# The PSUM bank kept for transposed k becomes a fourth shared bank, and the order of all instructions is made anew

## The chip, the cores and the metric

The kernel runs on one core of a Trainium2 chip. A core has five engines, each with its own queue of instructions that it works off strictly in order: TensorE (PE in the profile, with its weight loads as PEld), VectorE (DVE), ScalarE (ACT), GpSimd (POOL) and SyncE (SP), which here only issues DMAs. Matrix products are written to PSUM, which has eight banks of 128 partitions by 512 floats; DVE and ACT read them there. The metric is the time of one execution on the device in microseconds (us).

## The reference

Two stages follow each other for 4 sequences (B) of 768 tokens (S). The first is a recurrence over tokens with 8 heads of 48 elements, the second a gated feed-forward layer with a product over the sequence. Cut to what matters:

```python
for t in range(S):                                    # first stage, per head
    cur = einsum('bhd,bhe->bhde', u[None] * kt, vt)
    y[:, :, t] = einsum('bhd,bhde->bhe', rt, state + cur)
    state = wt[:, :, :, None] * state + einsum('bhd,bhe->bhde', kt, vt)

h = gelu(x @ w_in)                                    # x is y, (B, 768, 384); w_in 384 x 1024
u, v = h[..., :512], h[..., 512:]
v_n = (v - mean(v)) / sqrt(var(v) + 1e-06) * g_ln
v_s = einsum('ts,bsd->btd', w_sg, v_n) + b_sg[None, :, None]
return x + (u * v_s) @ w_out                          # w_out 512 x 384
```

## The kernel before, in words

The recurrence is cut into chunks of 128 tokens (`C`), six per sequence, 24 in all, numbered 0 to 23 in this text. For each chunk DVE runs two scans over the decay factors (`decays`, lines 445 and 450), DVE or POOL multiplies them into r and k (lines 452 and 474), PE transposes k (`turned_k`, line 521) and multiplies (`products`, lines 535 and 538), DVE masks the result (`masked`, line 556) and adds up the state (`state`, lines 571 and 579), and PE makes the chunk's output from both (`outputs`, lines 618 and 642). Line 592 or, on ACT, line 590 decays the state between chunks. `own_weights` gives the weight of each token for itself: from products on PE for the first six chunks (line 488), from two multiplications and a sum (lines 496, 498, 501) for the others; line 510 or, on ACT, line 508 spreads it over a diagonal.

The feed-forward layer needs its left factors in two parts, high and low, so each product is three matmuls (lines 721, 722 and 723). It goes by half sequences of 384 tokens: `split_x` makes the two parts of x (on PE with lines 710 and 711 for the first chunks, else by a subtraction in line 716), `v_piece` one product per chunk of 128 tokens, then GELU and the normalisation (lines 744 to 763), `u_piece` four products per half, `gate_piece` four products per half over all six chunks of v (weights `wsgh`, `wsgl`), each followed by DVE, DVE, ACT, DVE (lines 797, 799, 801, 803), and `out_piece` three products per half from the four gates. Weights come as 64-bit words; `f64_weight` splits them on DVE, and for the first ones also on PE (lines 856 to 858).

Every product that fills a PSUM bank takes one from the pool `m_m` (tiles `m_ps`) and gives it back when its last reader is done: a `v` or `u` product after the GELU on ACT, a gate product after line 803, an out product after line 819. The pool holds three banks before. Two banks belong to `a_ps`, two to `y_ps`, and one, `k_ps`, to the transposed k alone:

```python
    m_a = slots("a_ps", 1, [2, FF], at=ps)
    m_s = slots("k_ps", 1, [NP, C], at=ps)
    m_y = slots("y_ps", 1, [2, 256], [2, 256], at=ps)
    m_m = slots("m_ps", 3, [FF], at=ps)
```

The order of instructions on each queue is not written out. Each step is a generator that yields `Op`s, and `Plan.run` places them one after the other on the engine where they would end first, by assumed costs (`Op({"DVE": 0.6, "POOL": 1.15}, ...)` lets the planner choose), by the ranks of the steps (`LEAD`, `FIRST`, `PIECE`, `WEIGHT`) and by which buffers are free by its clock. An `Op` with `two=True` on DVE excludes POOL in the plan, and the reverse. What comes out is a fixed order on each queue and a fixed choice of engine and bank; on the chip only semaphores between producers and consumers hold instructions back.

Of the kernel before, what the change touches and what calls it, by code (L numbers as in the profile page):

```python
# [36 lines left out]
LEAD = (2.27, 1.56, 2.02, 2.02)  # L37
FIRST = {"v": -0.61, "u": 5.2, "gate": 4.9, "out": 9.02}
PIECE = {"v": 1.09, "u": 7.07, "gate": 7.71, "out": 2.93}
WEIGHT = {"v": -4.46, "u": -19.4, "sg0": 2.89, "sg1": 2.21, "out": -10.09, "g": 17.79}  # L40

BIAS = {"DVE": -0.0, "POOL": -0.09}
JOINED = 6

ON_PE = {"own": 6, "x": 5, "w": 8}
# [49 lines left out]
class Event:  # L95
    t = None
# [194 lines left out]
def rwkv_gmlp(ctx: ExitStack, tc: tile.TileContext, wpad, kr, vtok, ktok, vt, u, ucol, w_in, g_ln, w_sgT, b_sg, w_out, out):  # L291
    nc = tc.nc
# [4 lines left out]
    def copy(e, o, i):  # L297
        nc.scalar.copy(o, i) if e == "ACT" else engine[e].tensor_copy(o, i)  # L298
# [141 lines left out]
    def decays(n):  # L440

        x = ch[n]
        yield Op({"DVE": 1.15}, after=[x.e_W], done=x.e_suf, two=True)
        W, Suf = x.W, x.Suf
        nc.vector.tensor_tensor_scan(Suf[:, WL - 1:0:-1], W[:, WL - 1:0:-1], D1[:, WL - 1:0:-1], 0.0,  # L445
                                     ALU.mult, ALU.add)
        yield Op({"DVE": 0.12}, after=[ch[n - 1].e_pre] if n else [])
        nc.vector.reciprocal(D2[:, 0:WL - 1:Q], Suf[:, 1:WL - 1:Q])
        yield Op({"DVE": 1.15}, done=x.e_pre, two=True)
        nc.vector.tensor_tensor_scan(W[:, 0:WL - 1], W[:, 0:WL - 1], D2[:, 0:WL - 1], 0.0, ALU.mult, ALU.add)  # L450
# [20 lines left out]
    def decayed_k(n):  # L471
        x = ch[n]
        op = yield Op({"DVE": 0.6, "POOL": 1.15}, after=[x.e_KR, x.e_suf, *x.own], done=x.e_k, two=True)
        engine[op.e].tensor_tensor(cols(x.KR[:, 0]), cols(x.KR[:, 0]), blocks(x.Suf, 2), ALU.mult)
        x.w.done(op.seen)

    def own_weights(n):
# [15 lines left out]
        else:  # L493
            op = yield Op({"POOL": 1.05, "DVE": 0.47}, after=[x.e_RK, e_u], two=True)
            t = x.rk.tile
            engine[op.e].tensor_tensor(t[:, 0], t[:, 0], u_bc, ALU.mult)
            op = yield Op({"POOL": 1.05, "DVE": 0.47}, two=True)
# [4 lines left out]
        op = yield Op({"POOL": 1.0, "ACT": 1.92, "DVE": 0.6}, take=[s_a], done=x.e_A, free=[own], two=True)  # L502
# [10 lines left out]
    def turned_k(n):  # L513

        x = ch[n]
        m = T if steps[n][1] == NC - 1 else C
        op = yield Op({"PE": 0.37}, after=[x.e_k, *([ch[n - 1].e_kt] if n else [])], take=[m_s])
        kt_ps, = op.got
        x.kr.done(op.seen)
        for p in range(NP):  # L520
            nc.tensor.transpose(kt_ps.tile[0:m, p], x.KR[:, 0, p * C:p * C + m], ident)
# [36 lines left out]
    def state(n):  # L558
# [5 lines left out]
        op = yield Op({"DVE": 0.27} if g else {"DVE": 0.27, "ACT": 0.3}, after=[x.e_sd, *([x.e_S2] if g else [])],  # L564
# [9 lines left out]
        if not last:  # L574
            op = yield Op({"DVE": 0.27}, take=[s_S1], done=x.e_S1)
            x.S1, = op.got
            x.ps.done(op.seen)
            x.T2.done(op.seen)
            nc.vector.tensor_tensor(x.S1.tile, ds_ps(1), x.T2.tile[:, :, 0:D], ALU.add)

    def decayed(n):

        x, before = ch[n], ch[n - 1]
        op = yield Op({"DVE": 0.27, "POOL": 0.6, "ACT": 0.92}, after=[before.e_S1, x.e_pc], take=[s_S2], done=x.e_S2,
# [21 lines left out]
    def outputs(n):  # L606
# [29 lines left out]
        op = yield Op({"PE": 0.79 if g else 0.55}, small=True, after=[e_look, *final], done=x.e_ym, next_to=joined)  # L636
# [58 lines left out]
    def split_x(h_, g):  # L695
# [19 lines left out]
        op = yield Op({"DVE": 0.46, "POOL": 1.05}, done=h_.e_x[g], free=[h_.x], two=True)  # L715
# [9 lines left out]
    def v_piece(b, g):  # L725
# [29 lines left out]
        op = yield Op({"ACT": 0.85, "DVE": 0.46, "POOL": 0.95}, free=[sb])  # L755
# [74 lines left out]
    def f64_weight(src, hi, lo, done, rank, at, after, on_pe):  # L830
# [9 lines left out]
        yield Op({"DVE": 0.38 if n == FF else 0.3}, two=True)  # L840
# [9 lines left out]
        yield Op({"DVE": 0.59 if n == FF else 0.48}, free=[b_raw], two=True)  # L850
        nc.vector.scalar_tensor_tensor(lo if on_pe else f, words(raw, U32, 0), 2.0 ** -52, f, ALU.mult, ALU.mult)
        if on_pe:
            op = yield Op({"PE": 1.4 if n == FF else 1.1}, take=[m_m], after=[e_hi], free=[b_t])
# [29 lines left out]
    def f32_weight(src, hi, lo, done, after):  # L883
# [5 lines left out]
        op = yield Op({"POOL": 1.05, "DVE": 0.47}, done=done, free=[raw], two=True)  # L889
# [89 lines left out]
    cnt_ps = m_s.take().tile[0:1, 0, 0:1]  # L979
# [175 lines left out]
```

## Time and profile before

| what | us |
|---|---|
| median of 3 runs (lowest, highest) | 376.29 (375.42, 378.51) |
| the profiled execution | 379.16 |
| its span, first to last instruction | 377.5 |
| PE busy in the span | 350.0 (93%) |
| DVE busy | 288.7 (76%) |
| ACT busy | 190.9 (51%) |
| POOL busy | 88.3 (23%) |

Times in all tables and rows below are those of the one profiled execution, which was slower than the median. A row of the groups of instructions reads: line, engine, operation, tile written <- tiles read, shapes, count, then busy us, mean ns of one, and the idle time of its engine just before them. A row of the waits reads: engine, line, the engine and line waited for, us in total, times, the longest. PE's count of fp32 matmuls is two for one instruction of lines 488, 535, 538, 618, 642, 710 and 856, because each runs in two passes.

### The profile page before, as it was taken

What the parts mean: (1) busy time and instruction counts of PE and PEld (TensorE: products, weight loads), DVE (VectorE), ACT (ScalarE), POOL (GpSimd) and SP (SyncE); (2) the same over time, 40 slices, a digit from 0 to 9 for tenths busy, and PEclk for the clock granted to TensorE, in tenths of its full rate; (3) what the DMA queues carried; (4) which work ended last, traced back from release to release, by engine and by line L of the source; (5) the groups of instructions that cost most, each with busy time, mean ns of one, the idle gap of its engine ahead of it and who ended that gap; (6) DMA issues with size and microseconds to landing.
All of it is one profiled execution on the core that took longest, in us unless ns stands there. A gap on an engine that the chain in (4) does not pass through costs nothing.

```text
span 377.5 us, 10936 instructions
## 1 busy us (share of the span) xinstructions
PE 350.0 (93%) x4505; PEld 317.8 (84%) x4505; DVE 288.7 (76%) x577; ACT 190.9 (51%) x508; POOL 88.3 (23%) x118
## 2 busy tenths in 40 slices
PE   1988899998999998999986999999999999999994
PEld 1665768797998888899986988899999889999993
DVE  7999999999999999999988797675531655353151
ACT  2566886882544575874353156663246764411210
POOL 7121331224252364143402314230000122100000
PEclk9999999999999999999999899999999999999999
DMA  8686754681165436753355412140145501001001
GB/s 257 256 268 185 226 176 143 202 303 62 47 234 159 156 129 198 259 178 103 120 155 181 123 51 84 65 158 15 57 175 180 173 3 63 3 0 63 2 0 70
DMA packets 23961, 49.82 MB, mean 132 GB/s; under 512 B 3808, under 2 KB 12768, under 8 KB 23904
## 3 DMA queue, kind: packets, MB, share of 16 engines
q1 hardware_dynamic: 23904, 49.05, 39.5%
q8 instruction: 37, 0.61, 0.6%
q14 instruction: 20, 0.16, 0.1%
HBM read 43.14 MB, written 4.72 MB: 127 GB/s over the span
## 4 chain that ended last, share of the span: by engine, by line
PE 43%; DVE 22%; DMA 3%; issue 2%; ACT 1%; DVEq 0%; ACTq 0%
PE m_ps L721 13%; PE m_ps L723 12%; PE m_ps L722 12%; DVE W L445 3%; DVE xT L716 2%; DVE m_ps L797 2%; DVE W L450 2%; DMA KR<-in_w_in 2%; DVE a L556 1%; PE y_ps L618 1%; DVE vn L763 1%; DMA out<-o 1%; DVE own L501 1%; PE y_ps L642 1%; DVE m_ps L799 1%
## 5 line engine op out<-in xcount | busy, mean ns | idle before, releaser
L721 PE MATMUL m_ps<-wsgh,vn 128*128 128x384 f32 x192 | 66.5, 347 | 1.9 <-DVE g L803 1.9
L723 PE MATMUL m_ps<-wsgh,vn 128*128 128x384 f32 x192 | 65.8, 343 | 0.4 <-DVE vn L763 0.4
L722 PE MATMUL m_ps<-wsgl,vn 128*128 128x384 f32 x192 | 65.5, 341 | 0.0
L801 ACT CAST g<-m_ps 128x384 fp32r<-128x384 f32 x32 | 15.3, 479 | 63.3 <-DVE m_ps L799 63.3
L721 PEld LDWEIGHTS m_ps<-wsgh,vn 128*128 128x128 f32 x192 | 36.6, 191 | 3.1 <-DVE g L803 2.5
L797 DVE SCALAR_TENSOR_TENSOR m_ps<-m_ps,g_ln,b_bc 128x384 f32<-128x384 f32 x32 | 19.7, 620 | 25.5 <-PE m_ps L723 25.3
L723 PEld LDWEIGHTS m_ps<-wsgh,vn 128*128 128x128 f32 x192 | 36.6, 190 | 1.1 <-DVE vn L763 1.1
L722 PEld LDWEIGHTS m_ps<-wsgl,vn 128*128 128x128 f32 x192 | 36.5, 190 | 0.2
L721 PE MATMUL m_ps<-xT,winh 128*128 128x384 f32 x96 | 34.3, 357 | 0.0
L721 PE MATMUL m_ps<-g,wouth 128*128 128x384 f32 x96 | 33.3, 347 | 0.4 <-ACT v L744 0.4
L722 PE MATMUL m_ps<-g,wouth 128*128 128x384 f32 x96 | 32.5, 339 | 0.8 <-DVE g L803 0.8
L722 PE MATMUL m_ps<-xT,winh 128*128 128x384 f32 x96 | 32.4, 338 | 0.0
L723 PE MATMUL m_ps<-xT,winl 128*128 128x384 f32 x96 | 32.4, 338 | 0.0
L723 PE MATMUL m_ps<-g,woutl 128*128 128x384 f32 x96 | 32.4, 338 | 0.0
L461 ACT ACTIVATE junk<-W 128x1032 f32<-128x1032 f32 x24 | 25.6, 1067 | 13.0 <-DVE W L450 8.0
L445 DVE TENSOR_TENSOR_SCAN W<-W,D 128x516 f32<-128x516 f32 x24 | 30.9, 1286 | 1.7 <-DMA W<-in_wpad 1.7
L450 DVE TENSOR_TENSOR_SCAN W<-W,D 128x516 f32<-128x516 f32 x24 | 30.4, 1267 | 0.2
L721 PE MATMUL m_ps<-winh,xT 128*128 128x512 f32 x72 | 29.4, 408 | 0.6 <-DVE g L803 0.6
L752 POOL TENSOR_TENSOR st<-st,mhalf 128x1 f32<-128x1 f32 x24 | 17.9, 747 | 51.3 <-DVE st L750 44.2
L723 PE MATMUL m_ps<-winh,xT 128*128 128x512 f32 x72 | 28.6, 398 | 0.3 <-ACT xT L298 0.3
L722 PE MATMUL m_ps<-winl,xT 128*128 128x512 f32 x72 | 28.4, 394 | 0.0
L618 PE MATMUL y_ps<-a,vtok 64*64 64x64 f32 x768 | 21.6, 224 | 5.4 <-issue 4.5
(148 smaller groups left out, 819.1 us busy)
## 6 DMA issues: line engine op xcount, KB each, us to landing
KR<-in_kr SPq DMA_DIRECT2D x24, 512.0 KB, 4.4
RK<-in_ktok SPq DMA_DIRECT2D x18, 384.0 KB, 3.4
W<-in_wpad SPq DMA_DIRECT2D x24, 258.5 KB, 2.9
vtok<-in_vtok SPq DMA_DIRECT2D x24, 192.0 KB, 4.6
out<-o SPq DMA_DIRECT2D x21, 192.0 KB, 1.9
vn<-in_w_in SPq DMA_DIRECT2D x6, 512.0 KB, 6.2
KR<-in_w_in SPq DMA_DIRECT2D x6, 512.0 KB, 3.7
u<-in_w_sgT SPq DMA_DIRECT2D x12, 192.0 KB, 3.5
```

The source lines that it names most:

```text
L445: nc.vector.tensor_tensor_scan(Suf[:, WL - 1:0:-1], W[:, WL - 1:0:-1], D1[:, WL - 1:0:-1], 0.0, ALU.mult, ALU.add)
L450: nc.vector.tensor_tensor_scan(W[:, 0:WL - 1], W[:, 0:WL - 1], D2[:, 0:WL - 1], 0.0, ALU.mult, ALU.add)
L461: nc.scalar.activation(junk.rearrange("p (a x) -> p a x", a=2), both, AF.Square, accum_out=chk[:, n:n + 1])
L501: nc.vector.tensor_reduce(own.tile, t[:, 1].rearrange("p (h e) -> p h e", e=D), AX.X, ALU.add)
L618: nc.tensor.matmul(place(j, q, r, c_), x.V[64 * c_:64 * c_ + 64, h * D:h * D + 64], x.a.tile[64 * c_:64 * c_ + 64, j, p], start=(start and ...
L716: engine[op.e].tensor_tensor(xl[:, :, cs], x[:, :, cs], xh[:, :, cs].bitcast(F32), ALU.subtract)
L721: nc.tensor.matmul(ps, lh, rh, start=(i == 0), stop=False)
L722: nc.tensor.matmul(ps, lh, rl, start=False, stop=False)
L723: nc.tensor.matmul(ps, ll, rh, start=False, stop=(i == n - 1))
L752: nc.gpsimd.tensor_tensor(rstd, var, c.mhalf, ALU.pow)
L797: nc.vector.scalar_tensor_tensor(ps, ps, c.g[:, d:d + 1], c.b_bc[:, ts], ALU.mult, ALU.add)
L801: nc.scalar.copy(gh, ps)
```

## The change

The pool `k_ps` is dropped and `m_ps` has four banks. `turned_k` takes its bank from the pool that all other products use, and gives it back when the copy of the transposed k is done. The last chunk of x that PE splits is chunk 3 and no longer chunk 4. The ranks of the steps and the assumed costs have other numbers, so that the planner makes another order, and chooses other engines for some steps.

```diff
-LEAD = (2.27, 1.56, 2.02, 2.02)
...
+LEAD = (9.13, 0.32, 0.06, 0.01)
...
-ON_PE = {"own": 6, "x": 5, "w": 8}
+ON_PE = {"own": 6, "x": 4, "w": 8}
...
     m_a = slots("a_ps", 1, [2, FF], at=ps)
-    m_s = slots("k_ps", 1, [NP, C], at=ps)
     m_y = slots("y_ps", 1, [2, 256], [2, 256], at=ps)
-    m_m = slots("m_ps", 3, [FF], at=ps)
+    m_m = slots("m_ps", 4, [FF], at=ps)
...
-        op = yield Op({"PE": 0.37}, after=[x.e_k, *([ch[n - 1].e_kt] if n else [])], take=[m_s])
-        kt_ps, = op.got
+        op = yield Op({"PE": 0.37}, after=[x.e_k, *([ch[n - 1].e_kt] if n else [])], take=[m_m])
+        m_, = op.got
+        kt_ps = m_.tile.rearrange("t (p c) -> t p c", c=C)
...
-        op = yield Op({"ACT": 0.48, "DVE": 0.58}, take=[s_kt], free=[kt_ps], done=x.e_kt)
+        op = yield Op({"ACT": 0.48, "DVE": 0.58}, take=[s_kt], free=[m_], done=x.e_kt)
...
-        op = yield Op({"DVE": 0.59, "POOL": 1.15}, done=s_.e_v[g], free=[vb], two=True)
+        op = yield Op({"DVE": 0.7, "POOL": 1.2}, done=s_.e_v[g], free=[vb], two=True)
...
```

Line numbers of the changed kernel are one lower than before from line 353 to line 518, and the same elsewhere; in the text the old numbers are used, in the rows of the order each kernel has its own.

**The start, on PE.** The rows begin with the products of chunk 0 (line 538). `a_0_98` is the masked chunk 0, which line 618 waits for; lines 856 to 858 split the weights `winh`, `winl`. Before:

```order
L538 MATMUL a_ps_0_129<-vtok_0_85,kt_0_101 64x48 x16
L856 MATMUL m_ps_0_135<-vn_179,ident 128x512
L857 MATMUL m_ps_0_135<-winh,minus 128x512
L858 MATMUL m_ps_0_135<-winl,same 128x512
L856 MATMUL m_ps_0_133<-vn_182,ident 128x512
L857 MATMUL m_ps_0_133<-winh,minus 128x512
L858 MATMUL m_ps_0_133<-winl,same 128x512
L618 MATMUL y_ps_1_132<-a_0_98,vtok_0_85 64x64 x2
```

and now:

```order
L538 MATMUL a_ps_0_129<-vtok_0_85,kt_0_101 64x48 x16
L618 MATMUL y_ps_1_131<-a_0_98,vtok_0_85 64x64 x2
L618 MATMUL y_ps_0_130<-a_0_98,vtok_0_85 64x64 x2
L618 MATMUL y_ps_1_131<-a_0_98,vtok_0_85 64x64 x2
L618 MATMUL y_ps_0_130<-a_0_98,vtok_0_85 64x64 x2
L521 MATMUL m_ps_0_135<-ident,KR_0_83 128x128 x4
L856 MATMUL m_ps_0_132<-vn_179,ident 128x512
```

The two groups of three weight matmuls that stood ahead of the output of chunk 0 now stand behind it.

**The start, on DVE.** Line 556 is the mask of chunk 0; lines 843 to 851 split weights. Before:

```order
L845 SCALAR_TENSOR_TENSOR vn_182<-vn_181,vn_182 128x512
L851 SCALAR_TENSOR_TENSOR winl<-vn_178,vn_179 128x512
L849 TENSOR_SCALAR vn_182<-vn_182 128x512
L843 TENSOR_SCALAR vn_186<-vn_185 128x512
L851 SCALAR_TENSOR_TENSOR winl<-vn_181,vn_182 128x512
L845 SCALAR_TENSOR_TENSOR vn_186<-vn_185,vn_186 128x512
L556 COPY_PREDICATED a_0_98<-mask,a_ps_0_129 128x512
```

and now:

```order
L849 TENSOR_SCALAR vn_179<-vn_179 128x512
L845 SCALAR_TENSOR_TENSOR vn_182<-vn_181,vn_182 128x512
L556 COPY_PREDICATED a_0_98<-mask,a_ps_0_129 128x512
L579 TENSOR_TENSOR S_0_102<-a_ps_0_129,S_0_105 128x192
L851 SCALAR_TENSOR_TENSOR winl<-vn_178,vn_179 128x512
```

Five instructions that stood ahead of the mask now stand behind it.

**The fourth gate of the second sequence's first half, on PE.** `g_2704` before and `g_2749` now are that gate's two parts; the tiles `xT` are split halves of x, and their products with `winh` and `winl` at 384 columns are `u_piece`. Before:

```order
L721 MATMUL m_ps_0_134<-g_2704,wouth 128x384
L722 MATMUL m_ps_0_134<-g_2704,wouth 128x384
L723 MATMUL m_ps_0_134<-g_2704,woutl 128x384
L521 MATMUL k_ps_0_130<-ident,KR_0_82 128x128 x4
L721 MATMUL m_ps_0_135<-xT_2212,winh 128x384
L722 MATMUL m_ps_0_135<-xT_2212,winh 128x384
```

and now:

```order
L721 MATMUL m_ps_0_135<-g_2749,wouth 128x384
L722 MATMUL m_ps_0_135<-g_2749,wouth 128x384
L723 MATMUL m_ps_0_135<-g_2749,woutl 128x384
L521 MATMUL m_ps_0_132<-ident,KR_0_82 128x128 x4
L721 MATMUL m_ps_0_133<-xT_2623,winh 128x384
L722 MATMUL m_ps_0_133<-xT_2623,winh 128x384
```

`xT_2212` is the second half of the same sequence, `xT_2623` the first half of the next one. The 36 matmuls of the second half's `u` products stood behind this gate; now they stand ahead of it.

**A transpose between a gate and its use, on PE and DVE.** On PE, now: the last matmuls of the fourth gate product of the very first half (`vn_1110` is the sixth normalised v), then the transpose of chunk 6, then the first out product (`g_1206` is the first gate):

```order
L721 MATMUL m_ps_0_134<-wsgh,vn_1110 128x384
L722 MATMUL m_ps_0_134<-wsgl,vn_1110 128x384
L723 MATMUL m_ps_0_134<-wsgh,vn_1110 128x384
L521 MATMUL m_ps_0_135<-ident,KR_0_82 128x128 x4
L721 MATMUL m_ps_0_133<-g_1206,wouth 128x384
```

The transpose takes the bank `m_ps_0_135`. On DVE, now, the last reader of that bank is the first of these rows (line 803):

```order
L803 TENSOR_TENSOR g_1206<-m_ps_0_135,g_1206 128x384
L803 TENSOR_TENSOR g_1213<-m_ps_0_133,g_1213 128x384
L447 RECIPROCAL D_137<-W_0_81 128x4
L509 TENSOR_TENSOR a_0_98<-own_0_90,diag 128x512
L797 SCALAR_TENSOR_TENSOR m_ps_0_132<-m_ps_0_132,g_ln,b_bc 128x384
```

Before, that transpose wrote to `k_ps` and could follow whatever DVE did with the gates. Of the 24 transposes 6 now take a bank that a gate product held last, and 2 one that an out product held.

More of the change, by code (lines that the diff above doesn't have):

```diff
@@ L34 @@
 LIM = 1e30
-LEAD = (2.27, 1.56, 2.02, 2.02)
[L38 to L42, printed above, removed]
+LEAD = (9.13, 0.32, 0.06, 0.01)
+FIRST = {"v": -2.89, "u": 0.51, "gate": 5.3, "out": 9.31}
+PIECE = {"v": -15.16, "u": 7.49, "gate": 10.73, "out": 3.19}
+WEIGHT = {"v": -8.73, "u": -32.46, "sg0": 4.99, "sg1": 2.04, "out": -53.2, "g": 17.86}
+BIAS = {"DVE": 0.18, "POOL": 0.12}
 JOINED = 6
-ON_PE = {"own": 6, "x": 5, "w": 8}
+ON_PE = {"own": 6, "x": 4, "w": 8}
 FIRST_LOADS = {(0, "load_w"): -20.0, (0, "load_kr"): -19.0, (1, "load_w"): -17.0, (1, "load_kr"): -16.0,
@@ L442, in decays @@
         x = ch[n]
-        yield Op({"DVE": 1.15}, after=[x.e_W], done=x.e_suf, two=True)
+        yield Op({"DVE": 1.2}, after=[x.e_W], done=x.e_suf, two=True)
         W, Suf = x.W, x.Suf
@@ L448, in decays @@
         nc.vector.reciprocal(D2[:, 0:WL - 1:Q], Suf[:, 1:WL - 1:Q])
-        yield Op({"DVE": 1.15}, done=x.e_pre, two=True)
+        yield Op({"DVE": 1.18}, done=x.e_pre, two=True)
         nc.vector.tensor_tensor_scan(W[:, 0:WL - 1], W[:, 0:WL - 1], D2[:, 0:WL - 1], 0.0, ALU.mult, ALU.add)
@@ L472, in decayed_k @@
         x = ch[n]
-        op = yield Op({"DVE": 0.6, "POOL": 1.15}, after=[x.e_KR, x.e_suf, *x.own], done=x.e_k, two=True)
+        op = yield Op({"DVE": 0.65, "POOL": 1.2}, after=[x.e_KR, x.e_suf, *x.own], done=x.e_k, two=True)
         engine[op.e].tensor_tensor(cols(x.KR[:, 0]), cols(x.KR[:, 0]), blocks(x.Suf, 2), ALU.mult)
@@ L501, in own_weights @@
             nc.vector.tensor_reduce(own.tile, t[:, 1].rearrange("p (h e) -> p h e", e=D), AX.X, ALU.add)
-        op = yield Op({"POOL": 1.0, "ACT": 1.92, "DVE": 0.6}, take=[s_a], done=x.e_A, free=[own], two=True)
+        op = yield Op({"POOL": 1.05, "ACT": 1.95, "DVE": 0.7}, take=[s_a], done=x.e_A, free=[own], two=True)
         x.a, = op.got
@@ L574, in state @@
         if not last:
-            op = yield Op({"DVE": 0.27}, take=[s_S1], done=x.e_S1)
+            op = yield Op({"DVE": 0.29}, take=[s_S1], done=x.e_S1)
             x.S1, = op.got
@@ L583, in decayed @@
         x, before = ch[n], ch[n - 1]
-        op = yield Op({"DVE": 0.27, "POOL": 0.6, "ACT": 0.92}, after=[before.e_S1, x.e_pc], take=[s_S2], done=x.e_S2,
+        op = yield Op({"DVE": 0.4, "POOL": 0.7, "ACT": 0.92}, after=[before.e_S1, x.e_pc], take=[s_S2], done=x.e_S2,
                       two=True)
@@ L714, in split_x @@
             return
-        op = yield Op({"DVE": 0.46, "POOL": 1.05}, done=h_.e_x[g], free=[h_.x], two=True)
+        op = yield Op({"DVE": 0.54, "POOL": 1.05}, done=h_.e_x[g], free=[h_.x], two=True)
         engine[op.e].tensor_tensor(xl[:, :, cs], x[:, :, cs], xh[:, :, cs].bitcast(F32), ALU.subtract)
@@ L754, in v_piece @@
         engine[op.e].tensor_tensor(off, neg, rstd, ALU.mult)
-        op = yield Op({"ACT": 0.85, "DVE": 0.46, "POOL": 0.95}, free=[sb])
+        op = yield Op({"ACT": 0.85, "DVE": 0.55, "POOL": 0.95}, free=[sb])
         if op.e == "ACT":
@@ L839, in f64_weight @@
         e_t, e_hi = Event(), Event()
-        yield Op({"DVE": 0.38 if n == FF else 0.3}, two=True)
+        yield Op({"DVE": 0.46 if n == FF else 0.36}, two=True)
         t, f = tfs[:, 0].bitcast(I32), tfs[:, 1]
@@ L888, in f32_weight @@
         copy(op.e, hi, raw.tile)
-        op = yield Op({"POOL": 1.05, "DVE": 0.47}, done=done, free=[raw], two=True)
+        op = yield Op({"POOL": 1.15, "DVE": 0.54}, done=done, free=[raw], two=True)
         engine[op.e].tensor_tensor(lo, raw.tile, hi.bitcast(F32), ALU.subtract)
```

24 lines of the change are left out of this document (12 added, 12 removed).

## The prediction

> **What bounds the kernel now.** I read the page's head first, then the busy time in four stretches (columns: stretch, length, then busy us and instructions of PE, PE's weight loads, DVE, ACT, POOL, then clock and DMA).
>
> ```profile
> PE 350.0 (93%) x4505; PEld 317.8 (84%) x4505; DVE 288.7 (76%) x577; ACT 190.9 (51%) x508; POOL 88.3 (23%) x118
> 0.00:60.00 60.00, 47.26 (x819) 36.34 (x819) 56.21 (x105) 38.19 (x107) 20.32 (x37) 1.00 0.72 231
> 60.00:210.00 150.00, 141.71 (x2210) 128.83 (x2210) 145.09 (x282) 85.67 (x232) 48.03 (x48) 1.00 0.50 163
> 210.00:372.00 162.00, 161.07 (x1478) 152.62 (x1477) 86.99 (x192) 67.05 (x169) 19.95 (x33) 0.99 0.20 69
> 372.00:377.50 5.50, 0.00 (x0) 0.00 (x0) 0.45 (x1) 0.00 (x0) 0.00 (x0) 0.94 0.22 78
> ```
>
> PE is busy 350.0 us of 377.5; its 27.5 us of idle time lie so: 12.7 before 60, 8.3 from 60 to 210, 0.9 from 210 to 372, and 5.5 behind its last matmul. Up to 210 DVE is the fuller engine: idle 3.8 before 60 (nearly all before its first load lands), then 4.9 of 150 us. From 210 on PE runs alone through a backlog. So the front is paced by DVE, the back is pure PE time, and only PE's idle time in the front, and the amount of PE work, can be won.
>
> The chain of waits says the same. Three of its pieces in order of time (start, us, what), and the PE row of the first handover:
>
> ```profile
> 189.41 0.52 DVE g L803
> ...
> 198.72 1.93 DVE W L445
> ...
> 206.11 1.80 issue
> 189.99 0.44 PE L722 MATMUL m_ps<-g,wouth 128*128 128x384 f32 x1 [0.82 <-DVE g L803]
> ```
>
> Back from about 201 us the chain is nearly all DVE, ahead of it nearly all PE. PE takes over from DVE just behind the fourth gate of the second sequence's first half (line 803 at 189.41). Who PE waits for (the waits of PE, total us, times, longest):
>
> ```profile
> PE m_ps L488 <- DVE RK L484: 7.4, 1, 7.4
> PE y_ps L618 <- issue: 4.5, 2, 2.6
> PE m_ps L721 <- DVE g L803: 2.5, 4, 1.6
> PE k_ps L521 <- DVE KR L474: 1.3, 2, 0.9
> PE y_ps L618 <- DVE y L298: 1.0, 1, 1.0
> PE m_ps L710 <- DMA x<-y: 0.8, 1, 0.8
> PE m_ps L722 <- DVE g L803: 0.8, 1, 0.8
> PE y_ps L642 <- DVE look L298: 0.7, 1, 0.7
> ```
>
> The 7.4 is the start. The 4.5 of "issue" stand in the middle of a group of line 618 and end by nothing the profile shows; I leave them as they are. What DVE's lateness costs PE visibly behind the start is 2.5 + 1.3 + 1.0 + 0.8 + 0.7 = 6.3 us.
>
> **The change part by part.** *Less work ahead of DVE's late results.* At the fourth gate just named I counted, in both orders, what stands ahead of it on DVE. Line 450 goes from 19 to 18, line 474 from 12 to 10, line 496 from 6 to 3, line 498 from 6 to 4, line 592 from 6 to 2, line 759 from 8 to 6, and line 510 from 9 to 13; the planner gives these to POOL and ACT or places them later. The remaining differences are of one to three short instructions each and partly cancel, and I leave them out.
>
> ```profile
> L450 DVE TENSOR_TENSOR_SCAN W<-W,D 128x516 f32<-128x516 f32 x24 | 30.4, 1267 | 0.2
> L474 DVE TENSOR_TENSOR KR<-KR,W 128x512 f32<-128x512 f32 x17 | 12.6, 741 | 0.0
> L496 DVE TENSOR_TENSOR RK<-RK,u_bc 128x384 f32<-128x384 f32 x9 | 5.6, 626 | 0.0
> L498 DVE TENSOR_TENSOR RK<-RK 128x384 f32<-128x384 f32 x10 | 6.6, 662 | 0.0
> L592 DVE TENSOR_TENSOR S<-S,pc 128x192 f32<-128x192 f32 x9 | 4.8, 528 | 0.2
> L759 DVE TENSOR_SCALAR v<-v,st 128x512 f32<-128x512 f32 x17 | 10.1, 593 | 0.2
> L510 DVE TENSOR_TENSOR a<-own,diag 128x512 f32<-128x512 f32 x9 | 7.6, 840 | 0.0
> ```
>
> That is 1.27 + 2 × 0.741 + 3 × 0.626 + 2 × 0.662 + 4 × 0.528 + 2 × 0.593 − 4 × 0.840 = 5.9 us less DVE work ahead of this gate.
>
> *More PE work ahead of them.* On PE there stand 36 more matmuls of `u` and 9 more of `out` ahead of the first use of that gate. Their spacing comes from a stretch in which PE waits for nothing (first and last of 24 rows):
>
> ```profile
> 329.81 0.34 PE L723 MATMUL m_ps<-wsgh,vn 128*128 128x384 f32 x1
> ...
> 333.86 0.34 PE L722 MATMUL m_ps<-wsgl,vn 128*128 128x384 f32 x1
> ```
>
> Twenty-three steps in 4.05 us are 0.176 us each, 45 matmuls 7.9 us. PE now needs this gate later and DVE delivers it earlier: the two are 5.9 + 7.9 = 13.8 us further apart, less the 1.5 us of the next edit. So here DVE stops setting the pace, and the waits of 2.5 and 0.8 us for line 803 should go. With them I take the 1.3 for the multiplied k (DVE does 13 instead of 17 of these in all) and the 1.0 for the copy of y (2 instead of 7 on DVE). The 0.7 for the look at the output stays: 8 instead of 11 are on DVE, but PE waits for that round trip whichever engine makes it. Sum −5.6 us. The bounds are 0, if PE meets DVE elsewhere, and −6.3.
>
> *One split of x less on PE.* Lines 710 and 711 run for four chunks instead of five:
>
> ```profile
> L710 PE MATMUL m_ps<-x,ident 128*128 128x384 f32 x10 | 4.2, 503 | 0.8 <-DMA x<-y 0.8
> L711 PE MATMUL m_ps<-xT,minus 128*128 128x384 f32 x5 | 3.1, 613 | 0.0
> ```
>
> (4.2 + 3.1) / 5 = 1.5 us less on PE, −1.5 if PE sets the end from there on, 0 if it would have waited; I take −1.5. DVE exchanges a copy for one subtraction, which is nothing.
>
> *The start.* The mask of chunk 0 moves ahead of five DVE instructions, and the chunk's output on PE ahead of two groups of weight matmuls (lines 856 to 858):
>
> ```profile
> 13.34 1.05 PE L538 MATMUL a_ps<-vtok,kt 64*64 64x48 f32 x32
> 14.78 2.08 PE L856 MATMUL m_ps<-vn,ident 128*128 128x512 f32 x2 [0.39 <-DVE vn L845]
> 15.92 0.68 DVE L851 SCALAR_TENSOR_TENSOR winl<-vn,vn 128x512 fp32r<-128x512 uint32 x1
> 18.40 0.72 DVE L556 COPY_PREDICATED a<-mask,a_ps 128x512 f32<-128x512 uint8 x1
> 19.39 0.46 PE L618 MATMUL y_ps<-a,vtok 64*64 64x64 f32 x16
> ```
>
> The mask starts 18.40 − 15.92 = 2.5 us earlier, so line 618 starts at about 16.9 instead of 19.39. But PE then has done none of the weight work that took it from 14.78 to 19.39, 4.6 us. It is behind by 4.6 − 2.5 = 2.1 us at that point, and waits from 14.4 to 16.9. The same weight work later meets inputs that are ready: +0.7 if it then takes 3.2 us as a pair, which I infer from line 857 and 858 having waited inside these 4.6 us, +2.1 if not. I take +1.5, because DVE's lead in the first sequence grows only slowly.
>
> *The fourth bank and the loss of the kept one.* A gate holds its bank through four steps of DVE and ACT, so the fourth gate waits for line 803 of the first where there are three banks; part of the 2.5 us above is this, counted once. In exchange 8 of the 24 transposes now take a bank that a gate or an out product held. No row of before shows a transpose waiting for a bank. Bounds: 0 if it is free in time, and per transpose 1.6 us, the longest wait for line 803 above. I take 0 for the sum, since PE comes later to DVE's results everywhere behind chunk 6; the other end is a rival.
>
> *DMAs.* The number of transfers is the same (237 on SP before the end). SP's queue loads two decay factors earlier and two weights of `w_in` later; DMA is 0.72 busy before 60 us, so I give this ±1 us in the range and nothing in the sum.
>
> *The sum,* against the profiled execution's own time of 379.16 (span 377.5 and 1.7 around it): −5.6 − 1.5 + 1.5 = −5.6, or 373.6. The median of the runs stands at 376.29 / 379.16 = 0.992 of the profiled execution, so 376.29 − 5.6 = **370.7 us**.
>
> **The rivals.** *POOL takes back what it relieves DVE of: 375.0.* POOL gets more operations of two operands: line 474 from 7 to 11, 496 from 9 to 14, 498 from 8 to 11, and 510 from 10 to 5.
>
> ```profile
> L474 POOL TENSOR_TENSOR KR<-KR,W 128x512 f32<-128x512 f32 x7 | 10.0, 1425 | 10.6 <-DVE RK L484 5.4 <-DMA KR<-in_kr 4.3 <-DVE st L746 0.8
> L496 POOL TENSOR_TENSOR RK<-RK,u_bc 128x384 f32<-128x384 f32 x9 | 10.1, 1118 | 18.0 <-DVE x L298 13.8 <-DMA RK<-in_ktok 4.2
> L498 POOL TENSOR_TENSOR RK<-RK 128x384 f32<-128x384 f32 x8 | 9.5, 1190 | 1.7 <-DVE RK L496 1.4
> L510 POOL TENSOR_TENSOR a<-own,diag 128x512 f32<-128x512 f32 x10 | 12.0, 1198 | 39.4 <-PE y_ps L618 21.8 <-DVE own L501 16.3 <-ACT own L298 1.3
> 10.56 1.55 POOL L474 TENSOR_TENSOR KR<-KR,W 128x512 f32<-128x512 f32 x1 [3.02 <-DVE RK L484]
> 11.00 2.20 DVE L450 TENSOR_TENSOR_SCAN W<-W,D 128x516 f32<-128x516 f32 x1
> ```
>
> 4 × 1.425 + 5 × 1.118 + 3 × 1.190 − 5 × 1.198 = 8.9 us more on POOL. The scan that began beside a POOL operation took 2.20 us against a mean of 1.267, 0.93 lost beside 1.55 of POOL. At that rate 8.9 us cost DVE 5.3, and the 5.9 are gone. Against it: the 7.9 us of PE work moved ahead remain. If half of the 5.6 us of waits returns and the split's 1.5 is lost in them, 2.8 us of gain remain, less the start's 1.5: 376.29 − 1.3 = 375.0. For the rule behind the row: the Trainium skill, "SBUF — State Buffer", section "Who interferes with whom", says that a DVE instruction with two SBUF inputs contends with a GpSimd instruction that reads SBUF, and that the loser waits out the whole instruction. By that rule all 8.9 us could come back, an estimate, and the front would be DVE's again; the scan of 2.20 agrees with a wait of this kind, and the mean of 1.267 says that it is not the usual case.
>
> *More goes: below 367.* If the 4.5 us of "issue" also fall where PE is ahead, 370.7 − 4.5 = 366.2. Nothing in the order speaks for it, since PE is now the engine that sets the end.
>
> *Slower: transposes wait for their bank, 383.* PE works in order. A transpose whose bank a gate still holds stops everything behind it, among it the chunk's products, which DVE then waits for, which delays the next line 803. With all 8 at 1.6 us that is 12.8 us: 370.7 + 12.8 = 383.5. It decides for slower by 1% from (380.1 − 370.7) / 8 = 1.2 us per transpose on. For it: before, PE was kept by line 803 four times with three banks. Against it: those came where DVE was behind, and the transpose stands beside out products that need the same gates anyway, so most of such a wait would be there without it.
>
> *No change* would be that the waits for line 803 are only DVE's total work, which falls by few per cent; it gives 375 to 376.3.
>
> **How the numbers follow.** My forecast of 370.7, itself good for 367 to 373, has a chance of 0.53; POOL 0.16 and no change 0.10 (together 373 to 379); more (below 367) 0.08; slower by the banks or another wait of its kind (above 380) 0.13. The range goes from 365.5, the second case with 0.7 to spare, to 379.5: it leaves out little below and most of the slower case. Within 1% is 372.5 to 380.1, about what a measurement of this kernel can tell from no change (its runs lie within 375.42 to 378.51). Faster by over 1% takes 0.50 of the forecast's 0.53 and the 0.08, hence 0.58; within 1% 0.29; slower 0.13.
>
> **What would show it.** PE idle from 60 to 210 falls from 8.3 to 4 us or less, and no wait for line 803 is above 0.5 us in total there. PE waits about 2 us between 14 and 17 us. DVE's busy time falls to about 283 us (288.7 − 5.9); if it stays near 288, with lines 450 and 474 longer than their means above, POOL took it back. Rows of line 521 that wait for line 803 or 819 would be the slower case. It would be wrong altogether if the clock of PE fell below 0.99 for longer than before, or if DVE still ran without a gap until 210.

## The result, and the profile after

The changed kernel takes 373.06 us (median of 13 runs, 371.82 to 374.96). The kernel before, run 13 times beside it, takes 376.79 (375.3 to 381.09). The ratio is 0.9897 with a 95% interval of 0.9871 to 0.9924: faster by 1.0%, where 370.7 was forecast. Ratios leave out runs that fell into a slower state, and they are not the quotients of the medians given beside them. The profiled execution took 373.16 us with a span of 371.4. Lines 353 to 518 of the kernel before have a number lower by one in the kernel after; its rows carry its own numbers.

The head of the page after, and the busy time in stretches (stretch, length, then busy us and instructions of PE, PE's weight loads, DVE, ACT, POOL, then clock, DMA share and GB/s):

```profile
PE 348.5 (94%) x4502; PEld 318.9 (86%) x4502; DVE 284.7 (77%) x555; ACT 198.0 (53%) x529; POOL 96.1 (26%) x120
0.00:60.00 60.00, 48.05 (x845) 36.72 (x849) 52.97 (x98) 39.32 (x115) 21.34 (x37) 1.00 0.71 232
60.00:210.00 150.00, 146.03 (x2209) 135.75 (x2202) 141.22 (x266) 87.76 (x237) 53.19 (x50) 0.99 0.48 153
```

PE is idle 12.0 us before 60 (12.7 in the kernel before) and 4.0 from 60 to 210 (8.3 before). DVE is no longer the fuller engine in the front: 141.2 of 150 us against PE's 146.0, where it had 145.1 against 141.7.

The waits of PE, in us, how often, the longest:

```profile
PE m_ps L487 <- DVE RK L483: 7.4, 1, 7.4
PE y_ps L618 <- DVE a L556: 2.3, 1, 2.3
PE y_ps L642 <- ACT look L298: 1.7, 1, 1.7
PE y_ps L618 <- issue: 1.5, 2, 1.4
PE m_ps L723 <- ACT xT L298: 1.1, 1, 1.1
PE y_ps L642 <- DVE look L298: 0.6, 1, 0.6
```

Every wait for line 803, for the multiplied k and for the copy of y is gone. One of 2.3 us for the first mask is new, and the two for ACT have grown: for the look at the output from 0.5 to 1.7 us, for a half of x from 0.3 to 1.1.

The end shows what the prediction doesn't speak of. First the last rows of PE and of DVE in the kernel after:

```profile
363.97 0.34 PE L723 MATMUL m_ps<-g,woutl 128*128 128x384 f32 x1
364.24 0.19 PE L980 MATMUL m_ps<-junk,ones 128*1 128x1 f32 x2
364.35 0.56 DVE L819 TENSOR_TENSOR u<-m_ps,x 128x384 f32<-128x384 f32 x1 [1.55 <-PE m_ps L723]
364.82 0.14 DVE L981 TENSOR_SCALAR bad<-m_ps 1x1 int32<-1x1 f32 x1
```

Then the same two places in the kernel before, the check's product and PE's last row:

```profile
327.12 0.19 PE L980 MATMUL k_ps<-junk,ones 128*1 128x1 f32 x2
371.52 0.34 PE L723 MATMUL m_ps<-g,woutl 128*128 128x384 f32 x1
```

Line 980 is the product that sums the checks of the input's range; line 981 compares it, and the branch behind line 982 waits for that value. In the kept bank it ran 44 us ahead of PE's last row. In a shared bank it comes last, and the time from the end of PE's last row to the end of the span grows from 377.5 − 371.86 = 5.64 us to 371.4 − 364.43 = 6.97.

So the 6.1 us between the two spans divide thus: PE's idle time before 210 us −5.1 (21.0 to 15.9), its idle time between 210 and its last row −0.8, its busy time −1.5, the end +1.3.

### The profile page after: what moved, and what is told of

It is laid out like the page before. It is cut to its first block, busy times and chain, and to the rows that moved or that the text cites. A ratio compares the mean times of both kernels' runs of the same rounds, so it can differ in the third digit from the quotient of the medians.

```text
span 371.4 us, 10943 instructions
## 1 busy us (share of the span) xinstructions
PE 348.5 (94%) x4502; PEld 318.9 (86%) x4502; DVE 284.7 (77%) x555; ACT 198.0 (53%) x529; POOL 96.1 (26%) x120
## 4 chain that ended last, share of the span: by engine, by line
PE 80%; DVE 12%; DMA 2%; ACT 2%; issue 1%; SPq 1%; ACTq 0%; DVEq 0%
PE m_ps L721 22%; PE m_ps L723 21%; PE m_ps L722 20%; PE y_ps L618 3%; PE y_ps L642 3%; PE a_ps L535 3%; DVE W L449 2%; PE m_ps L521 2%; PE a_ps L538 2%; DVE W L444 2%; PE m_ps L856 1%; DVE KR L451 1%; DVE a L556 1%; DMA vn<-in_w_in 1%; SPq L689 1%
## 5 line engine op out<-in xcount | busy, mean ns | idle before, releaser
L752 POOL TENSOR_TENSOR st<-st,mhalf 128x1 f32<-128x1 f32 x24 | 18.9, 791 | 61.6 <-DVE st L750 46.1
L473 POOL TENSOR_TENSOR KR<-KR,W 128x512 f32<-128x512 f32 x11 | 16.8, 1531 | 45.0 <-DVE RK L483 18.0
L722 PE MATMUL m_ps<-winl,xT 128*128 128x512 f32 x72 | 28.4, 394 | 0.0
```

The costliest lines, as they stand in the source:

```text
L722: nc.tensor.matmul(ps, lh, rl, start=False, stop=False)
L752: nc.gpsimd.tensor_tensor(rstd, var, c.mhalf, ALU.pow)
```

## The experiments

Twelve kernels were run, each in five rounds beside the kernel before; a ratio is always to that kernel, in brackets its 95% interval. Kernels with added lines have later lines at higher numbers.

**The check's product, early again.** The kernel after with one line changed:

```diff
-    cnt_ps = m_m.take().tile[0:1, 0:1]
+    cnt_ps = m_a.take().tile[0:1, 0, 0:1]
```

> The kernel after, with the one-element product of the check (line 980) in the bank of a_ps, which nothing uses behind the last chunk; all else, the order too, stays but for this product's place on PE, which comes some 137 rows earlier. Theory 'tail': behind PE's last matmul the kernel after spends 7.1 us and the one before 5.6, because the product, its comparison on DVE and the load of its value come one after another behind the last product; then this kernel takes 373.06 - 1.5 = 371.6 us, and the time from PE's last matmul to the span's end is 5.6 us again. Rival 'no tail': the 1.5 us belong to the last output's way out and the check lies beside it; then 373.1 and 7.1 us.

Measured: 371.49 us, ratio 0.987 (0.9838 to 0.9903). PE's last row in its trace:

```profile
363.39 0.34 PE L723 MATMUL m_ps<-g,woutl 128*128 128x384 f32 x1
```

It ends at 363.73, the span at 369.4: 5.7 us, as in the kernel before. I call this kernel "the kernel after with the early check"; most of what follows starts from it.

**The check's product, late in the kernel before.**

```diff
-    cnt_ps = m_s.take().tile[0:1, 0, 0:1]
+    cnt_ps = m_m.take().tile[0:1, 0:1]
```

> The kernel before, with the check's product in one of the three shared banks, which puts it last on PE; nothing else moves on PE. Theory 'tail': 376.8 + 1.5 = 378.3 us, and 7.1 instead of 5.6 us from PE's last matmul to the span's end. Rival 'no tail': 376.8.

Measured: 377.4 us, ratio 1.0039 (1.0004 to 1.0074), which is 1.5 us with an interval of 0.2 to 2.8. Two rows of its trace, from the end and from its waits:

```profile
370.80 0.19 PE L980 MATMUL m_ps<-junk,ones 128*1 128x1 f32 x2
```
```profile
PE y_ps L618 <- issue: 2.2, 1, 2.2
```

From 370.99 to the span's end at 378.0 are 7.0 us. The four traces agree: where the check comes last, the end takes 1.3 to 1.4 us longer. The total times are less sharp. The two ratios of the kernel after, 0.9897 and 0.987, lie 1.0 us apart and their intervals overlap; in the kernel before the ratio says 1.5 us, the medians beside each other, 377.4 and 377.32, say nothing. The second row serves further below.

**The bank alone.** The kernel before with four shared banks and the transposes in them; its numbers stay, and the check goes to `m_a`:

```diff
-    m_s = slots("k_ps", 1, [NP, C], at=ps)
-    m_m = slots("m_ps", 3, [FF], at=ps)
+    m_m = slots("m_ps", 4, [FF], at=ps)
...
-        op = yield Op({"PE": 0.37}, after=[x.e_k, *([ch[n - 1].e_kt] if n else [])], take=[m_s])
+        op = yield Op({"PE": 0.37}, after=[x.e_k, *([ch[n - 1].e_kt] if n else [])], take=[m_m])
```

> The kernel before with four shared banks and no kept one, all numbers (ranks, costs, splits of x) as before; the check's product stands in a_ps, so that it is early as before. The order is made anew by the old numbers with the new banks. Theory 'the numbers did it' (the prediction: the bank is worth nothing by itself): 376.8 within 2 us, and PE still waits for lines 803 or 474 for 3 us or more behind the start. Rival 'the bank did it': a gate no longer waits for line 803 of the third gate ahead, so the waits for line 803 (3.3 us before) go by the bank alone, and the time is 376.8 - 3.7 - 1.5 = 371.6.

Measured: 375.54 us, ratio 0.9987 (0.9951 to 1.0024): no change that can be told. Its waits for line 803:

```profile
PE m_ps L721 <- DVE g L803: 1.0, 1, 1.0
PE m_ps L722 <- DVE g L803: 0.7, 2, 0.4
PE m_ps L521 <- DVE g L803: 0.3, 1, 0.3
```

They fall from 3.3 to 2.0 us, and a transpose (line 521) waits for a bank for 0.3.

**The numbers alone.** The kernel after with the banks of before; the check is in the kept bank:

```diff
+    m_s = slots("k_ps", 1, [NP, C], at=ps)
-    m_m = slots("m_ps", 4, [FF], at=ps)
+    m_m = slots("m_ps", 3, [FF], at=ps)
...
-        op = yield Op({"PE": 0.37}, after=[x.e_k, *([ch[n - 1].e_kt] if n else [])], take=[m_m])
+        op = yield Op({"PE": 0.37}, after=[x.e_k, *([ch[n - 1].e_kt] if n else [])], take=[m_s])
```

> The kernel after with three shared banks and the kept one of before, all numbers as after; the check's product has the kept bank and is early. The order is made anew by the new numbers with the old banks. Theory 'the numbers did it': 371.6 us (373.1 less the late check's 1.5) within 1 us, with DVE's waits on PE's side below 1 us as in the kernel after. Rival 'the bank did it': 375 or more, with waits of PE for line 803 of 2 us or more behind 60 us.

Measured: 375.49 us, ratio 0.9984 (0.9954 to 1.0015). My theory, that the numbers did it, is missed: neither half alone moves the time, and the two together, with the check early as in both of these, give 0.987. The rival is not borne out either: PE waits for line 803 only 0.6 us here. This trace shows more. Of the 5.6 us of waits that the prediction counts as gone only 1.3 are left in it (0.6 for line 803, 0.7 for the multiplied k), and still PE's idle time ahead of its last matmul is 22.0 us, where the kernel before has 21.8 and the kernel after 15.9: other waits, for the first mask, for ACT and for a transfer, took their place. That those waits go is not enough; no others must come. Whether bank and numbers need each other, or whether each of these orders is only another throw, is taken up below.

**More work on DVE, in both kernels.** Behind each copy under the mask one sum that nobody reads:

```diff
         nc.vector.copy_predicated(x.a.tile.rearrange("s j p t -> s j (p t)"), mask, x.ps.tile[:, :, 0:NP * T])
+        nc.vector.tensor_reduce(pad, D2[:, 0:384], AX.X, ALU.add)
```

In the kernel after with the early check:

> The kernel after with the early check, and behind each of the 24 copies under the mask (line 556) one sum over 128x384 elements on DVE that nobody reads, about 0.4 us each (a row of 128x512 with one input took 0.40), so 9.6 us in all, some 16 to 18 of them, 6.4 to 7.2 us, while chunks are still worked on ahead of 200 us. Theory 'DVE stopped setting the pace': PE leads DVE nowhere by much less than this, so less than half shows: 371.5 + at most 3 = 374.5 or below. Rival 'DVE still paces the front': nearly all of it shows, 377.5 to 379.

In the kernel before:

> The kernel before with the same 24 sums on DVE. Theory 'DVE set the pace before': the 6.4 to 7.2 us that lie ahead of the fourth gate of the second sequence show nearly in full, 382.5 to 384, and PE's waits for line 803 grow by as much. Rival 'DVE did not set the pace': below 379.

The sums took longer than I had estimated. Their group (line, engine, operation, count, then busy us and mean ns), first in the kernel after, then in the kernel before:

```profile
L558 DVE TENSOR_REDUCE pad<-D 128x1 f32<-128x384 f32 x24 | 12.8, 534 | 0.0
```
```profile
L558 DVE TENSOR_REDUCE pad<-D 128x1 f32<-128x384 f32 x24 | 12.9, 536 | 0.0
PE m_ps L723 <- DVE g L805: 2.9, 4, 2.1
PE m_ps L724 <- DVE g L805: 1.2, 1, 1.2
```

The 16 to 18 sums of the front are 8.6 to 9.6 us. The kernel before pays 1.0208 (1.0149 to 1.0267), 7.8 us, most of them; five of its six runs had a granted clock of 0.991 or less, and the sixth, at 0.999, took 381.87 us. The kernel after pays 374.76 − 371.49 = 3.3 us (its ratio goes from 0.987 to 0.9948, interval 0.9912 to 0.9983), about a third. So DVE's work counted for more in the order before than it does now. One expectation fell: the waits for that gate (line 805 here) grew from 3.3 only to 4.1 us, and the kernel with the late check, whose order is that of before and which has no sums, shows 4.1 as well. In the traces the contrast is also weaker than in the medians: PE's idle time ahead of its last matmul grows by 3.0 us in the kernel before and by 1.7 in the kernel after, its busy time by 3.0 and 1.8. Of the busy time 1.7 us in each pair are one more stretch of PE at half its clock, of which the last section tells.

**The split of x for five chunks, as before.**

```diff
-ON_PE = {"own": 6, "x": 4, "w": 8}
+ON_PE = {"own": 6, "x": 5, "w": 8}
```

> The kernel after with the early check, and the split of x on PE for five chunks as before instead of four. Theory 'PE sets the end': lines 710 and 711 cost PE 1.5 us more, so 373.0. Rival 'PE would have waited': 371.5 within 0.7.

Measured: 367.01 us (366.73 to 367.78), ratio 0.974 (0.9697 to 0.9783). This gives PE the 1.5 us of work back that the change had taken off it, and the kernel is 4.5 us faster than its base. Neither theory has room for that. The stretches of its trace from 60 us on:

```profile
60.00:150.00 90.00, 89.58 (x1265) 1.00 0.51 161
150.00:210.00 60.00, 59.83 (x990) 1.00 0.52 161
```

(Columns here: PE's busy time, clock, DMA share, GB/s.) PE has 0.6 us of idle time left in 150; the waits for the look at the output, 2.3 us in the kernel after, are gone. Over the whole trace PE's idle time ahead of its last matmul is 12.9 us against 17.4 in the base, as much as the gain. What came with it is another order: from about the fifth chunk's split on (62 to 66 us), the planner decides differently on all engines. One split was changed in the source, and the rest of the program in the order.

**Two changes of a number that change no work.** To see what a remade order is worth by itself, POOL's handicap of 0.12 became 0.11 in one kernel, and the planner's cost of a split of x went from 0.82 to 0.84 in the other, both from the kernel after with the early check:

```diff
-BIAS = {"DVE": 0.18, "POOL": 0.12}
+BIAS = {"DVE": 0.18, "POOL": 0.11}
```
```diff
-            op = yield Op({"PE": 0.82}, take=[m_m], free=[h_.x])
+            op = yield Op({"PE": 0.84}, take=[m_m], free=[h_.x])
```

> The kernel after with the early check, and one number of the planner moved by 0.01: POOL's handicap of 0.12 is 0.11. The work is the same (the same matmuls, the same splits); where a choice between POOL and DVE tips, the order from there on is made anew. Theory 'a remade order is worth some us by itself, whatever the edit': the time lies 2 us or more from 371.5, to either side, and then the 4.5 us that five instead of four splits of x gained, and the differences of the bank alone and the numbers alone, can't be read as the price of these edits. Rival 'equal work gives equal time': 371.5 within 1.

> The kernel after with the early check, and the planner's cost of the two matmuls of a split of x at 0.84 instead of 0.82 us; the work is the same. A second look at the same question: by the theory 'a remade order is worth some us by itself' 2 us or more from 371.5, or from the first of these two; by the rival 371.5 within 1.

Measured: 375.29 us with ratio 0.993 (0.9903 to 0.9956), and 381.02 us with ratio 1.0103 (1.006 to 1.0145). By the medians the first is 3.8 us slower than its base, the second 9.5, with the same matmuls in all three (x4502); by the ratios, which set each beside the kernel before, it is 2.3 and 8.8, and the interval of the first only just touches that of its base. A part of the 9.5 is a lower granted clock; its run with the highest, 0.994, took 378.9 us, still 7.4 above the base. Three waits of the second that its base doesn't have at this size:

```profile
PE m_ps L521 <- DVE g L803: 1.9, 1, 1.9
PE m_ps L721 <- ACT xT L298: 1.6, 1, 1.6
PE m_ps L721 <- ACT vn L298: 1.3, 1, 1.3
```

The first of them is a row of the slower rival of the prediction, a transpose kept by a gate's bank. Four shared banks alone don't make it; it takes an order that happens to put the two together. With a scatter of this size between orders of equal work, the 4.5 us of the fifth split, and the nothing of bank alone and numbers alone, can't be read as prices of those edits. What they show is that the gain belongs to the banks and all the numbers together: with the banks of before, or with one number off by 0.01, about half of it or more is gone. How much a fourth bank is worth with numbers made for it stays open.

**More work on POOL.** In the order of the kernel after with the early check, with two additions that nobody reads behind each copy under the mask:

```diff
+        for _ in range(2):
+            nc.gpsimd.tensor_tensor(pad, D1[:, 0:192], D1[:, 192:384], ALU.add)
```

> The kernel after with the early check, in the same order, and on POOL two additions of 128x192 elements behind each of the 24 copies under the mask, which nobody reads: 48 at about 0.65 us, some 31 us more of POOL with two inputs. Theory 'POOL costs DVE a part': from the kernel after, in which POOL had 7.8 us more and DVE's busy time fell by 4.0 instead of 5.9, 1.9 / 7.8 = 0.25 us of DVE per us of POOL, so DVE's busy time rises by 7 to 8 us, and the time by about 2 to 3 us (24 sums on DVE, 12.8 us in all, cost 3.3). Rival 'POOL takes it all back' at the rate of the scan of the start (0.93 of 1.55): DVE busy +18 us, the time 378 or more. Rival 'no cost': DVE busy within 1 us, the time 371.5 within 1.

Measured: 373.25 us, ratio 0.9917 (0.9883 to 0.9952), 1.8 us above its base by the medians. DVE's busy time rose from 284.6 to 290.9. The additions, and two groups of DVE beside them:

```profile
L559 POOL TENSOR_TENSOR pad<-D 128x192 bf16<-128x192 f32 x48 | 42.2, 878 | 2.0
L766 DVE TENSOR_TENSOR vn<-v,vn 128x512 fp32r<-128x512 f32 x24 | 18.9, 793 | 1.9 <-ACT vn L298 1.9
L452 DVE TENSOR_TENSOR KR<-KR,W 128x512 f32<-128x512 f32 x18 | 15.2, 843 | 1.6 <-DMA KR<-in_kr 1.6
```

Without the additions the last two groups are:

```profile
L763 DVE TENSOR_TENSOR vn<-v,vn 128x512 fp32r<-128x512 f32 x24 | 16.2, 683 | 1.9 <-ACT vn L298 1.9
L451 DVE TENSOR_TENSOR KR<-KR,W 128x512 f32<-128x512 f32 x18 | 13.1, 725 | 0.9 <-DMA KR<-in_kr 0.8
```

POOL does cost DVE time, 6.3 us for 42.2, which is 0.15 us per us: less than my 0.25, and a quarter of the 0.6 of the one scan on which the rival in the prediction stood.

**PE kept at work at the start.** Matmuls that nobody reads, in PE's two idle stretches ahead of the first output:

```diff
     make_identity(nc, ident)
+    idle_a, idle_y = m_a.free[0][1], m_y.free[0][1][1]
+    for _ in range(16):
+        nc.tensor.matmul(idle_a[:, 0, 0:128], ident, ident, start=True, stop=True)
...
+        if n == 0:
+            for _ in range(10):
+                nc.tensor.matmul(idle_y[:, 1], ident, D1[:, 0:256], start=True, stop=True)
```

> The kernel after with the early check, and matmuls that nobody reads in PE's two idle stretches of the start: 16 of 128x128 ahead of the first product of chunk 0 (idle to 7.44 us), and 10 of 128x256 in the wait for the first mask (14.4 to 16.7). In the kernel after PE's rows from 16.68 to 22.92 us take about twice as long as the same lines later (line 521: 1.11 against 0.66; the pair of line 856: 1.91 against 1.10): 6.2 us for work that takes 3.5 by the spacing of the later rows. Theory 'the start costs PE time because its wait for the mask makes it run slowly afterwards': the rows behind the mask then have their later durations, and 371.5 - 2.7 = 368.8. Rival 'DVE paces the start': the rows are short, but PE then waits for DVE and the time stays 371.5 within 0.7. Rival 'slow for another reason' (operands, the DMA): the rows stay at 1.11 and 1.91.

Measured: 369.24 us, ratio 0.9804 (0.9754 to 0.9854), 2.3 us below its base by the medians. The rows behind the first mask, first in the kernel after (start, us, what), then with the filling matmuls (line 618 is 624 there, 521 is 524, 856 is 862):

```profile
13.34 1.05 PE L538 MATMUL a_ps<-vtok,kt 64*64 64x48 f32 x32
16.68 0.71 PE L618 MATMUL y_ps<-a,vtok 64*64 64x64 f32 x16 [2.29 <-DVE a L556]
17.32 1.11 PE L521 MATMUL m_ps<-ident,KR 128*128 128x128 f32 x4
18.23 1.91 PE L856 MATMUL m_ps<-vn,ident 128*128 128x512 f32 x2
...
20.93 0.71 PE L642 MATMUL y_ps<-KR,S 64*64 64x64 f32 x16
21.41 0.65 PE L618 MATMUL y_ps<-a,vtok 64*64 64x64 f32 x16
21.99 1.50 PE L856 MATMUL m_ps<-vn,ident 128*128 128x512 f32 x2
22.92 0.80 PE L857 MATMUL m_ps<-winh,minus 128*128 128x512 f32 x1
23.89 0.69 PE L535 MATMUL a_ps<-KR 64*64 64x64 f32 x32
```
```profile
12.03 0.63 PE L541 MATMUL a_ps<-vtok,kt 64*64 64x48 f32 x32
17.10 0.46 PE L624 MATMUL y_ps<-a,vtok 64*64 64x64 f32 x16
17.50 0.66 PE L524 MATMUL m_ps<-ident,KR 128*128 128x128 f32 x4
17.99 1.02 PE L862 MATMUL m_ps<-vn,ident 128*128 128x512 f32 x2
...
21.56 0.69 PE L538 MATMUL a_ps<-KR 64*64 64x64 f32 x32
```

The same instructions take 1.11 and 0.66, 1.91 and 1.02. The start of the kernel after cost PE time because it ran slowly behind the waits; with the waits filled it reaches chunk 1's products (line 535, 538 there) at 21.56 instead of 23.89. The kernel before has slow rows at its start too (2.08 us for line 856 at 14.78, in the prediction's rows), behind a wait of 0.4. In the trace of the base with the early check, whose rows stand in the last section, the slow stretch happens to be shorter and that point lies at 22.05, so there the filling shows only 0.5 us of the 2.3 between the medians. That idle stretches made these rows slow is shown; that the rows are all of the 2.3 us is not, and the intervals of the two ratios overlap by a little.

**The two that gained, together.** Five splits and the filling matmuls, the diffs above.

> The kernel after with the early check, five splits of x on PE, and the filling matmuls of the start. The split gave 367.0 and the filling 2.3 us from 371.5. Theory 'the two add up': 364.7 within 1 us, the fastest of all. Rival 'the fuller PE only meets DVE sooner': 366 to 367.

Measured: 365.3 to 369.5 us in five runs, of which the middle one took 367.16, and 371.46 in a sixth at a granted clock of 0.977, which the ratio of 0.9725 (0.9676 to 0.9775) leaves out. The five splits alone have 0.974: the two don't add up. One wait of its trace:

```profile
PE m_ps L716 <- DMA x<-y: 3.1, 2, 2.5
```

PE reaches the split of x sooner and stands there 2.5 us for the transfer of x. Behind this wait the granted clock is 0.50 from 32 to 38 us and partly so in the slices on both sides; by the clock's column that is 3.4 us of PE's time. This trace is of the run of 369.5 us, and the run of 365.3 had a mean clock of 0.997 instead of 0.989. Five splits with the early check, 367.01 us, and this one are both faster than the kernel before and after; which of the two is the faster isn't settled.

## Why the prediction was right, and where it wasn't

**Direction and main cause: right for this order.** DVE paced the front, and the order took it out of PE's way. The four waits that were to go, 2.5 + 0.8 + 1.3 + 1.0 = 5.6 us, are all gone, and the 0.7 for the look, which was to stay, is 0.6. PE's idle time from 60 to 210 fell to 4.0 us, the bound that I had set. The added sums bear the cause out, 7.8 us of about 9 paid before and 3.3 after, though less clearly in PE's idle time. But the numbers alone took most of these waits away too and gained nothing, so the forecast also needed that no other waits come in their place, which it didn't argue. Here some did: ACT's grew by 2.0 us. None of the signs of being wrong came: while PE worked, the clock fell below 0.99 for 3.4 us in each of the two traces, and DVE's idle time from 60 to 210 grew from 4.9 to 8.8 us.

**Left out: the check's product, +1.3 to 1.5 us.** This is the step that failed. The part on "the fourth bank and the loss of the kept one" counts the 24 transposes as all that used the kept bank. Line 979, in the diff, uses it too, and by the loss of the bank its product moves from 327 us to the very end. With it the sum is −5.6 + 1.5 = −4.1; measured −3.7. That the two are so close is partly luck, since the waits for ACT, the start and the "issue" came out otherwise than the sum has them.

**From the profile to the median.** For the profiled execution I forecast 379.16 − 5.6 = 373.6, and it took 373.16. I then carried the whole gain over to the median. But the profiled execution of before lay 2.4 us above its median and that of after 0.1, so part of the 6.0 us between the profiles was that one execution's own. What part can't be told from one trace. Traced again, with the check late in the one and early in the other, the two orders differ by 3.5 us in PE's idle time ahead of its last matmul (20.9 and 17.4) and not by the 5.9 of the first pair. Of the 4.5 us of "issue" in the first profile, which I left as they are, the trace of the kernel with the late check has 2.2, and the kernel after has 1.5.

**The start, forecast +1.5: more at first, and then mostly gone.** The mask came as worked out (wait of 2.3 us, first output at 16.68 instead of 16.9). The two groups of weight products took 2.70 (18.23 to 20.93) and 1.90 (21.99 to 23.89), 4.6 us again, not the 3.2 that the lower end assumed. I had put their length down to inputs that were not ready; the filling matmuls show that PE itself ran slowly. When both kernels have done three groups and the same products, before stands at about 25.5 us and after at 28.4: 2.9 us, beyond the upper bound of 2.1. But then before waits 2.65 us in a group of line 618, one of the two waits of "issue" that I left as they are, and after only 0.5. With the same rows behind them they stand at 30.4 and 31.0 us, in the second pair of traces at 30.8 and 29.6. So the two terms, the start and the untouched "issue", were both wrong, and their errors cancel for the most part.

**One split less, −1.5: not settled.** Lines 710 and 711 fell from 7.3 to 5.8 us, as worked out. PE's busy time fell by 1.5 as well, which says less: it also changes with the slow rows from trace to trace (348.5 us in the kernel after, 346.3 in the same order with the early check). But putting the split back made the kernel 4.5 us faster, with another order. The term holds for the two orders as they are, and says nothing about the edit.

**The fourth bank, 0: right for this order.** No transpose waits for line 803 or 819 in the kernel after. The rival of 1.6 us per transpose isn't empty: in another order of the same work one took 1.9, and the granted clock was 0.50 for 3 us behind it.

**POOL takes it back: the mechanism is there, its size was wrong.** DVE's busy time fell by 4.0 us instead of 5.9. Its multiplied k (line 474 before, 473 after) stretched from 741 to 865 ns, 13 × 0.124 = 1.6 us; that POOL did this is argued from the experiment above, not shown for these rows:

```profile
L473 DVE TENSOR_TENSOR KR<-KR,W 128x512 f32<-128x512 f32 x13 | 11.2, 865 | 0.0
L473 POOL TENSOR_TENSOR KR<-KR,W 128x512 f32<-128x512 f32 x11 | 16.8, 1531 | 45.0 <-DVE RK L483 18.0 <-DVE W L444 12.4 <-DMA RK<-in_ktok 10.2
```

PE no longer waits for it, so this cost nothing that a wait shows. The measured rate is 0.15 us of DVE per us of POOL. The Trainium skill, "SBUF — State Buffer", section "Who interferes with whom", has the loser wait out the whole instruction: that it loses agrees; how long one loser waits can't be read from means over instructions that meet one of these 48 additions and those that meet none.

## What to carry to other kernels

Where a planner makes the order, price the finished order row by row and not the edit: numbers moved by 0.01 and 0.02, with no change of work, cost 2.3 to 3.8 and 8.8 to 9.5 us here, where the whole change gained 3.7. So a change to such a kernel is compared over several neighbouring orders before its idea is credited. And follow every user of a resource that goes away down to the last instruction of the program: a product of 0.19 us made the end 1.3 us longer because it had become the last.

## What the runs showed of the hardware

PE ran at about half its rate at the start, until it had been at work for a while, and the profile's clock column doesn't show it there: it reads 1.00 over these stretches. The four transposes of a chunk took 1.11 us and later 0.66. Behind the wait for the first mask this lasted about 6 us in the kernel after (16.68 to 22.92) and about 3 us in the same order with the early check, of whose trace these are some rows:

```profile
16.25 0.71 PE L618 MATMUL y_ps<-a,vtok 64*64 64x64 f32 x16 [2.29 <-DVE a L556]
17.80 1.71 PE L856 MATMUL m_ps<-vn,ident 128*128 128x512 f32 x2
19.90 0.46 PE L642 MATMUL y_ps<-KR,S 64*64 64x64 f32 x16
22.05 0.69 PE L535 MATMUL a_ps<-KR 64*64 64x64 f32 x32
```

The Trainium skill, "TensorE: Matmul & The Clock Gate", Part 1 on the clock gate, states that the array runs at half clock until a window of about 3.4 us has been busy, and that the window runs freely, so that the count varies from run to run. The 3 and 6 us here agree with that, and so do the short rows from the start on, once the idle stretches were filled.

Later in the same traces the clock column does show such stretches, which in stretches of 60 or 150 us look like a clock of 0.97 or 0.99. Two rows of the kernel after, a wait and a matmul behind it:

```profile
116.99 0.69 PE L642 MATMUL y_ps<-KR,S 64*64 64x64 f32 x32 [1.66 <-ACT look L298]
119.23 0.52 PE L723 MATMUL m_ps<-wsgh,vn 128*128 128x384 f32 x1
```

In slices of 1 us the granted clock is 0.50 from 119 to 121, with 0.68 ahead of it and 0.62 behind; matmuls of 384 columns take 0.52 us there instead of 0.34 and start every 0.32 us instead of every 0.176. That is 3.4 us at half rate or 1.7 us lost, an estimate from these figures. The kernel before has one such stretch, from 209.8 to 213.0 us, behind a wait of 1.8 us, so between these two traces it cancels. The trace with the early check has the same wait of 1.66 us and no such stretch behind it. So behind the same wait of under 2 us such a stretch came in one execution and not in another; that the wait calls for it is likely, and no experiment here shows it for these later stretches.

The granted clock goes with the spread of the kernel after with the early check: its runs took 370.7 to 372.0 us at a mean clock of 0.995 or more, and 373.3 to 374.5 at 0.991 or less; 1.7 us in 370 are 0.005 of the mean. The kernel before, in the same rounds, shows this less clearly: at 0.997 or more its runs lie between 375.3 and 378.1.
